# Attention block: the normalised output is stored one key step later, and one weight preparation step per quad is left out

## The chip, the cores and the metric

The kernel runs on one core of one Trainium2 chip. The metric is the device time of one execution in microseconds, the median over several runs. Lower is better. The names of the engines are those of the profile: PE (TensorE) does the matmuls, DVE, ACT and POOL are the vector, scalar and general engines, and SP issues every DMA of this program.

## What is computed

A transformer block with adaptive layer norm: multi-query attention (32 query heads of 18 columns, one key and one value head) and an MLP, over 2048 tokens of 576 features, in fp32.

```
mod = (silu(c) @ w_mod).reshape(c.shape[0], 6, 1, -1)
sa, ca, ga, sb, cb, gb = (mod[:, 0], mod[:, 1], ..., mod[:, 5])
h = layernorm(x) * (1 + ca) + sa
x = x + ga * A(h)      # q,k,v = h@wq, h@wk, h@wv; p = softmax(q k^T * 18**-0.5); (p v) @ wo
h = layernorm(x) * (1 + cb) + sb
x = x + gb * B(h)      # gelu(layernorm(h) @ w1 + b1) @ w2 + b2, with 4608 hidden features
```

## The kernel before

**Stages.** Stage 1 (up to about 134 us) projects q, k and v. Stage 2 (134 to 1422 us) is attention. Stage 3 (1422 us to the end) first adds the output projection of the last 512 tokens and then runs the MLP in 36 passes `v`.

**Quads and key steps.** Attention goes over 32 quads `n`: 4 blocks of 512 tokens times 8 groups `qd` of four heads. A quad has 16 key steps `kc` of 128 keys. For each key step PE makes the scores (L824), ACT takes their exponentials into a tile `P` (L826), and PE multiplies by the values (L813) into the PSUM tile `psC`. In between PE computes the plain scores of a later quad once more (L322, L834) so that DVE finds each query's maximum (L846, L844). Those maxima of quad n+1 are gathered at key steps 12 and 13 of quad n (`smax_fin1`, `smax_fin2`). `smax_fin2` writes them into a small tile `ms`, and four DMAs (L367) put `ms` as extra rows into the query tile `qst` of quad n+1. The first score matmul of quad n+1 reads `qst`. These four DMAs are called the ms DMAs below.

**What sets the order.** The order on each engine is the order in which the code calls it; nothing is reordered by a scheduler. `between(n, kc)` is called once after each key step, and draws one step of several Python generators, in this order: `smax_fin1` or `smax_fin2`, then the `post_quad` of the quad before (in the list `posts`), the load of a later quad's queries, on odd key steps a step of `fill` (output projection and second layer norm of finished token blocks), and last a step of `prep`.

**post_quad.** When quad n is done, its output goes from PSUM to a tile `O` (L619, ACT). In the key steps of quad n+1 the four softmax sums are fetched out of `O` by DMA (L637, tile `R`), inverted (L641), sent to DRAM (L643, `dsum`) and read back broadcast over the partitions (L647, tile `T`). At key step 8 POOL multiplies `O` by `T` (L651). At key step 9 POOL splits the product into two parts in the tile `os` (L661, L662). Some key steps later four DMAs store `os` into `ATT` (L668, `big<-os`), the left operand of the output projection (L597). Four heads of quad 30 lie in chunk k = 3 of `ATT` for the last token block. Quads 0 to 2 and 31 take another path, without these sums by DMA.

**prep.** From quad 3 on, `prep` draws one step of `weight_parts` per key step. It scales w2 (L728), makes sums of w1 and w2 blocks (L730, L754), and splits each into two parts in a tile `r2`, of which there are two buffers (L694 and L695, the function `two`). The DMA that stores a split (`store`, L699) is issued when the next step is drawn. The blocks of w2 are loaded by L705 (tiles `r4` and `w2b`), and those of w1 for four of the 18 groups by L739 and L741 (tiles `r1` and `r4`; `r1` shares its memory with `w2b`). At key step 8 of quad 31 a loop draws whatever is left of `prep`, and then the first MLP weights are loaded (`load_w1`, L683, eight DMAs into `w1a`).

**The end of attention.** After the last quad PE runs `wo_tile` for three token tiles with k = 0 to 3 (L597), and then the last chunk and the first MLP products (L1040).

Of the kernel before, what the change touches and what calls it, by code (L numbers as in the profile page):

```python
# [30 lines left out]
def block_kernel(ctx: ExitStack, tc, x, wqkv, wo, w1, b1, w2, b2, c, wmod, ident_in, out):  # L31
# [277 lines left out]
    def load_q(n):  # L309
        tb, qd = divmod(n, NQ)  # L310
        if n not in QST:
            new_q(n)
        q = QST[n]
        for g in range(2):
            for r in range(3):
                src = qscr[tb, r // 2, 4 * DH * qd:4 * DH * (qd + 1), :]
                src = src.rearrange("(p g d) t -> g d p t", p=2, g=2)[g]
                sy.dma_start(q[64 * g + DH * r:64 * g + DH * (r + 1)].bitcast(F32), src)
# [30 lines left out]
    def smax_fin1(n):  # L349
        m = MR[n] = pa.tile([128, 16], F32, name="mxf", bufs=2)  # L350
        mm = MX.pop(n)
        if n == 0:
            ve.tensor_reduce(m, mm, axis=AX.X, op=ALU.max)
        else:
            ve.tensor_reduce(m[:, :8], mm[:, :8, :], axis=AX.X, op=ALU.max)
            ve.tensor_reduce(m[:, 8:], mm[:, 8:, :3], axis=AX.X, op=ALU.max)

    def smax_fin2(n):
        p = psB()
        pe.transpose(p[:16, :128], MR.pop(n), ident)  # L360
        ms = pa.tile([16, 2, 128], F32R, name="ms")
        ac.activation(ms[:, 0], p[:16, :128], AF.Copy, scale=-1.0)
        ve.scalar_tensor_tensor(ms[:, 1], p[:16, :128], -1.0, ms[:, 0].bitcast(F32), op0=ALU.mult, op1=ALU.subtract)
        for g in range(2):
            for s in range(2):
                r = 64 * g + R3 + s
                sy.dma_start(QST[n][r:r + 1].rearrange("o p (t c) -> o (p t) c", c=128).bitcast(F32),  # L367
                             ms[8 * g:8 * (g + 1), s].bitcast(F32))
# [205 lines left out]
    def ln2_block(tb):  # L574
        if "b" not in B2:
            B2["b"] = b2_scaled(load_b2())
        if tb % 2 == 0:
            YR[tb // 2] = per.tile([128, 2 * KD, TB], F32, name="yr", tag="big", bufs=3)
        for t in range(NT):
            yield from ln2_tile(tb, t)  # L580
        if tb % 2:
            R = YR[tb // 2]
            po.tensor_tensor(R[:, 5:7], R[:, 7:9], R[:, 5:7], op=ALU.subtract)
            yield
            po.tensor_tensor(R[:, 5:7], R[:, 5:7], R[:, 0:2], op=ALU.add)
            yield
# [16 lines left out]
    def wo_block(tb):  # L603
        for t in range(NT):
            for h2 in range(2):
                p = psB()
                wo_mm(tb, t, h2, p, 0, KD)
                wo_add(tb, t, h2, p)
                yield
# [3 lines left out]
    def post_quad(n, PV):  # L613

        tb, qd = divmod(n, NQ)
        last = n == NQT - 1 or n < 3
        e = ve if n == NQT - 1 else po
        O = px.tile([128, TB], F32, name="O")
        ac.activation(O, PV, AF.Copy)  # L619
        yield  # L620
        if last:
            yield
            T = px.tile([128, 16, 32], F32, name="T")
            ve.transpose(T.rearrange("p a b -> p (a b)"), O)
            yield
            R = px.tile([128, 16], F32, name="R", bufs=2)
            ve.reciprocal(R, T[:, :, DH])
            e.tensor_tensor(T, T, R[:, :, None].to_broadcast([128, 16, 32]), op=ALU.mult)
            yield
            if e is po:  # L630
                yield
            ve.transpose(O, T.rearrange("p a b -> p (a b)"))
            yield
        else:
            R = px.tile([128, 16], F32, name="R", bufs=2)
            for j in range(4):
                sy.dma_start(R[32 * j:32 * (j + 1)], O[32 * j + DH:32 * j + DH + 1].rearrange("o (c i) -> o c i", i=16))  # L637
            yield
            yield
            yield  # L640
            ve.reciprocal(R, R)  # L641
            yield
            sy.dma_start(dsum[n % 2].rearrange("j (c i) -> (j c) i", i=16), R)  # L643
            yield
            T = px.tile([128, TB], F32, name="T")
            for j in range(4):
                sy.dma_start(T[32 * j:32 * (j + 1)], dsum[n % 2, j:j + 1].to_broadcast([32, TB]))  # L647
            yield
            yield
            yield  # L650
            po.tensor_tensor(O, O, T, op=ALU.mult)  # L651
            yield
        A = ATT[tb].rearrange("p (s k) t -> p s k t", s=2)
        if qd == NQ - 1:
            os = A[:, :, KD - 1, :]
        else:
            os = px.tile([128, 2, TB], F32R, name="os")
        if last:
            ac.activation(os[:, 0], O, AF.Copy)
        else:  # L660
            po.tensor_copy(os[:, 0], O)  # L661
        e.tensor_tensor(os[:, 1], O, os[:, 0].bitcast(F32), op=ALU.subtract)  # L662
        if qd < NQ - 1:
            for _ in range(3):
                yield
            for j in range(4):
                k, r = divmod(4 * qd + j, HC)
                sy.dma_start(A[DH * r:DH * (r + 1), :, k, :].bitcast(F32), os[32 * j:32 * j + DH].bitcast(F32))  # L668
        yield
# [8 lines left out]
    def load_w1(i, what, save=False):  # L678
        for w in what.split():
            a = 4 * OPS.index(w) if w in OPS else 28  # L680
            b = min(a + 4, 31)
            ends = W1["r"][:, a:b].bitcast(F32), w1scr[i, :, a:b]
            sy.dma_start(*(ends[::-1] if save else ends))  # L683
# [108 lines left out]
    def step(q):  # L792
        if q:
            try:
                next(q[0])
            except StopIteration:
                q.popleft()
# [8 lines left out]
    def pv_mm(n, kc, h0, h1):  # L806

        if kc == 0 and h0 == 0:
            PVt[n] = psC()
        t = P.pop((n, kc)) if h1 == 4 else P[n, kc]  # L810
        cs = slice(128 * h0, 128 * h1)
        for j in range(4):
            pe.matmul(PVt[n][32 * j:32 * (j + 1), cs], V[:, kc, :], t[:, j, cs],  # L813
                      start=(kc == 0 and h0 == 0), stop=(kc == 15), skip_group_check=True)
        if kc == 15 and h1 == 4:
            gen = post_quad(n, PVt.pop(n))
            next(gen)
            posts.append(gen)
# [29 lines left out]
    def between(n, kc):  # L848

        if kc == 12 and n + 1 < NQT:  # L850
            smax_fin1(n + 1)
        if kc == 13 and n + 1 < NQT:
            smax_fin2(n + 1)
        for gen in list(posts):
            if next(gen, 0) == 0:
                posts.remove(gen)
        if kc == 1 and n >= 1 and n + 2 < NQT:
            load_q(n + 2)
        if kc == 12 and n % NQ == 0 and n:
            fill.append(wo_block(n // NQ - 1))  # L860
            if n // NQ - 1 < 2:
                fill.append(ln2_block(n // NQ - 1))
        if kc % 2:
            step(fill)
        if n > 2 and kc not in (11, 12):
            step(prep)
        if kc == 8 and n == NQT - 1:
            while prep:
                step(prep)
            W1["r"] = per.tile([128, 40, 128], F32R, name="w1a", tag="big", bufs=3)  # L870
            load_w1(0, " ".join(OPS) + " tails")

    for d in range(8 * NQT):
        n, kd = divmod(d, 8)
        if kd == 0 and n % NQ == 0:
            ATT[n // NQ] = big()
        un = units.get(d)
        ns, nm, np_ = [0, 0], [0, 0], 0
        for tok in MIX if un else PLAIN:
            if tok in "PH":  # L880
                s, h0 = 2 * d + np_ // 4, np_ % 4
                np_ += 4 if tok == "P" else 2
                if s:
                    pv_mm(*divmod(s - 1, 16), h0, (np_ - 1) % 4 + 1)
                if np_ % 4 == 0:
                    between(n, s % 16)
                continue
            g = int(tok[1])
            if tok[0] == "s":
                st_mm(n, 2 * kd + ns[g] // 2, g, ns[g] % 2)  # L890
                ns[g] += 1
            else:
                mx_mm(*un, tok[0], g, nm[g])
                nm[g] += tok[0] == "m"
# [469 lines left out]
```

## Time and profile before

| | |
|---|---|
| median of 3 runs | 2301.75 us (2300.64 to 2305.29) |
| the profiled execution | 2300.77 us, span 2299.0 us |
| PE busy | 2261.0 us, 98% of the span |
| DVE, ACT, POOL busy | 1685.6, 1486.5, 1351.4 us |
| mean granted clock of PE | 0.998 |

Times in the profile are microseconds from the start of the span. In a row of the timeline stand the start, the duration, the engine (SPq is SP issuing a DMA), the line of the code, the operation, the tile written and the tiles read, and in brackets how long the engine had been idle and what ended that. In a row of waits stand the total, the number of times and the longest. In a row of windows stand the length, the busy time of an engine with its number of instructions in brackets, the granted clock as a share of the full one, and the DMA engines' share.

### The profile page before, as it was taken

Reading aid. Unit: us, or ns where it says so; the run is one execution under the profiler, and the core shown is the slowest. Engines: PE = TensorE matmul, PEld = TensorE weight load, DVE = VectorE, ACT = ScalarE, POOL = GpSimd, SP = SyncE. Lnnn points to the kernel's source line nnn. Section 1 sums busy time; section 2 is a strip of 40 time slices with the busy share of each in tenths; the row PEclk is TensorE's granted clock in tenths of the full one; section 3 lists DMA queues with packets and bytes.
Section 4 is the critical chain, followed back from the end, with each engine's and each line's share of the span. In section 5 each row is a group of like instructions: output and inputs, shape, how many; then the busy total and the mean of one; then the engine's idle time right before and its main releaser. Section 6 shows DMA issues by size and latency. Waiting matters only on the chain.

```text
span 2299.0 us, 44576 instructions
## 1 busy us (share of the span) xinstructions
PE 2261.0 (98%) x16310; PEld 1414.3 (62%) x16310; DVE 1685.6 (73%) x3004; ACT 1486.5 (65%) x2851; POOL 1351.4 (59%) x1554
## 2 busy tenths in 40 slices
PE   8999999999999999999999999999999999999999
PEld 5644434454344454344454344899999999989898
DVE  6589999979899979999879992444444456666665
ACT  5569999979999969999979998322222232222221
POOL 6534556345566425657324332588888767777776
PEclk9999999999999999999999999999999999999999
DMA  6221223222222212223123232444444456666663
GB/s 221 87 99 48 76 88 108 89 81 66 75 79 83 92 55 84 83 69 104 60 64 98 73 97 83 162 153 172 149 153 172 147 165 194 181 177 184 178 183 124
DMA packets 160411, 267.73 MB, mean 116 GB/s; under 512 B 26955, under 2 KB 67787, under 8 KB 160193
## 3 DMA queue, kind: packets, MB, share of 16 engines
q1 hardware_dynamic: 160193, 264.89, 36.7%
q8 instruction: 129, 2.11, 0.4%
q14 instruction: 89, 0.73, 0.1%
HBM read 163.45 MB, written 92.24 MB: 111 GB/s over the span
## 4 chain that ended last, share of the span: by engine, by line
PE 92%; ACT 2%; issue 0%; DVE 0%; DMA 0%; SPq 0%; POOL 0%; ACTq 0%
PE psC L813 24%; PE psB L1040 18%; PE psB L824 12%; PE psA L1151 10%; PE psM L322 10%; PE psA L1120 8%; PE psB L834 4%; PE psB L597 2%; ACT P L826 1%; ACT O L619 1%; PE psA L597 1%; PE psB L152 0%; PE psB L251 0%; PE psB L360 0%; DMA qst<-ms 0%
## 5 line engine op out<-in xcount | busy, mean ns | idle before, releaser
L826 ACT ACTIVATE P<-psB 128x512 f32<-128x512 f32 x2048 | 1048.8, 617 | 7.7 <-PE psB L824 6.4
L846 DVE TENSOR_REDUCE mx<-psM 128x1 f32<-128x512 f32 x1476 | 945.6, 683 | 72.1 <-PE psB L824 28.2
L813 PE MATMUL psC<-P,V 128*32 128x256 f32 (+1 forms) x6056 | 599.4, 467 | 13.2 <-ACT O L619 13.2
L824 PE MATMUL psB<-qst,KS 64*128 64x512 f32 x2048 | 598.6, 435 | 5.1 <-DMA qst<-ms 4.7
L322 PE MATMUL psM<-KS,qst 64*128 64x512 f32 x1722 | 592.2, 432 | 0.0
L824 PEld LDWEIGHTS psB<-qst,KS 64*128 64x128 f32 x2048 | 301.3, 185 | 174.4 <-issue 77.6
L1040 PE MATMUL psB<-ops,w1a 128*128 128x512 f32 x1512 | 390.6, 396 | 0.0
L322 PEld LDWEIGHTS psM<-KS,qst 64*128 64x128 f32 x1722 | 283.9, 185 | 115.2 <-DVE mx L844 92.6
L1040 PEld LDWEIGHTS psB<-ops,w1a 128*128 128x128 f32 x1512 | 271.6, 188 | 47.7
L813 PEld LDWEIGHTS psC<-P,V 128*32 128x32 f32 x6056 | 119.7, 108 | 236.9 <-issue 212.1
L1151 PE MATMUL psA<-w2s,big 128*128 128x288 f32 x1488 | 255.4, 295 | 0.0
L1055 ACT ACTIVATE yr<-psB,b1t 128x512 f32<-128x512 f32 x72 | 49.6, 689 | 287.2 <-PE psB L1040 147.1
L1151 PEld LDWEIGHTS psA<-w2s,big 128*128 128x128 f32 x1488 | 221.3, 188 | 6.7
L837 ACT ACTIVATE xc<-psB 128x512 f32<-128x512 f32 x246 | 147.5, 600 | 90.8 <-PE psM L322 61.6
L1155 DVE TENSOR_TENSOR XT<-psA,XT 128x576 f32<-128x576 f32 x152 | 114.2, 752 | 121.5 <-PE psA L1151 121.4
L1055 ACT ACTIVATE gx<-psB,b1t 128x512 f32<-128x512 f32 x72 | 49.6, 689 | 225.8 <-PE psB L1040 76.5
L844 DVE CUSTOM_DVE_ANT_0 xc<-psM,xc 128x512 f32<-128x512 f32 x246 | 167.0, 679 | 4.1 <-PE psM L322 3.4
L1126 DVE TENSOR_TENSOR XT<-psA,XT 128x576 f32<-128x576 f32 x170 | 128.7, 757 | 32.8 <-PE psA L1120 23.5
L834 PEld LDWEIGHTS psB<-KD,qst 64*128 64x128 f32 x246 | 45.1, 183 | 159.2 <-ACT P L826 109.8
L132 POOL MEMSET qst<- 32x1024 f32 x62 | 58.6, 946 | 137.2 <-PE psB L824 91.8
L1059 POOL TENSOR_TENSOR big<-gx,big 128x512 fp32r<-128x512 f32 x72 | 94.8, 1316 | 63.4 <-ACT big L1058 49.6
L834 PE MATMUL psB<-KD,qst 64*128 64x512 f32 x246 | 122.4, 498 | 0.0
(197 smaller groups left out, 2978.1 us busy)
## 6 DMA issues: line engine op xcount, KB each, us to landing
w1a<-w1scr SPq DMA_DIRECT2D x154, 256.0 KB
w1scr<-w1a SPq DMA_DIRECT2D x98, 256.0 KB
w2scr<-r SPq DMA_DIRECT2D x72, 288.0 KB
w2sum<-r SPq DMA_DIRECT2D x68, 288.0 KB
w2s<-w2sum SPq DMA_DIRECT2D x68, 288.0 KB
w2s<-w2scr SPq DMA_DIRECT2D x29, 576.0 KB
qst<-qscr SPq DMA_DIRECT2D x192, 72.0 KB
w2s<-w2scr SPq DMA_DIRECT2D x34, 288.0 KB
```

The costliest lines, as they stand in the source:

```text
L322: pe.matmul(o, QST[n][64 * g:64 * g + 64, p, 128 * qt:128 * (qt + 1)], KS[64 * g:64 * g + 64, 512 * kb:512 * (kb + 1)], start=True, stop=True)
L813: pe.matmul(PVt[n][32 * j:32 * (j + 1), cs], V[:, kc, :], t[:, j, cs], start=(kc == 0 and h0 == 0), stop=(kc == 15), skip_group_check=True)
L824: pe.matmul(t, KS[64 * g:64 * g + 64, 128 * kc:128 * (kc + 1)], QST[n][64 * g:64 * g + 64, i, :], start=True, stop=True)
L826: ac.activation(P[n, kc][:, 2 * i + g, :], t, AF.Exp, scale=SCALE)
L834: pe.matmul(t, QST[n][64 * g:64 * g + 64, p, 128 * qt:128 * (qt + 1)], KD1[64 * g:64 * g + 64, :], start=True, stop=True)
L837: ac.activation(XC[-1], t, AF.Relu)
L844: ve.tensor_tensor_reduce(c, t, c, 1.0, -3.0e38, ALU.add, ALU.max, o)
L846: ve.tensor_reduce(o, t, axis=AX.X, op=ALU.max)
L1040: pe.matmul(o, x, y, start=(first and i == 0), stop=(i == len(terms) - 1), skip_group_check=True)
L1120: pe.matmul(p[:, i, :288], x[:, ts_], W2S[k][:, y], start=(bool(first) and q == 0), stop=(q == 2), skip_group_check=True)
L1126: ve.tensor_tensor(o, p[:, :, :288], o, op=ALU.add)
L1151: pe.matmul(p[:, nn, :288], x, y, start=(q == 0), stop=(q == len(terms) - 1))
```

## The change

The generator `post_quad` yields four times instead of three between the split and the store for n > 2, so the four `big<-os` DMAs are issued at key step 13 instead of 12. Since `smax_fin2` runs ahead of `posts` at key step 13, its ms DMAs now stand ahead of them on SP. And `prep` is no longer drawn at key step 10, as it was not at 11 and 12 before.

```diff
@@ post_quad
         if qd < NQ - 1:
-            for _ in range(3):
+            for _ in range(4 if n > 2 else 3):
                 yield
             for j in range(4):
...
@@ between
-        if n > 2 and kc not in (11, 12):
+        if n > 2 and kc not in (10, 11, 12):
             step(prep)
         if kc == 8 and n == NQT - 1:
             while prep:
                 step(prep)
```

In the rows of the order below an engine's instructions stand as they are queued: line, operation, output<-inputs, shape, and xN for several in a row. A number after `r_` is a buffer's number and means nothing else.

SP, ahead of quad 12 (key steps 8 to 15 of quad 11), before:

```order
L647 DMA T<-dsum 32x512 x4
L699 DMA w2scr<-r_8013 256x1x288
L699 DMA w2sum<-r_8085 128x576
L699 DMA w2scr<-r_8161 256x1x288
L668 DMA big<-os 18x2x512 x4
L367 DMA qst<-ms 1x8x128 x4
L699 DMA w2sum<-r_8308 128x576
L637 DMA R<-O 32x1x16 x4
```

And now:

```order
L647 DMA T<-dsum 32x512 x4
L699 DMA w2scr<-r_8066 256x1x288
L367 DMA qst<-ms 1x8x128 x4
L668 DMA big<-os 18x2x512 x4
L699 DMA w2scr<-r_8142 256x1x288
L699 DMA w2sum<-r_8331 128x576
L637 DMA R<-O 32x1x16 x4
```

The ms DMAs have moved ahead of the four stores of `os` and of the prep store that was drawn at key step 10. It is the same ahead of quads 5 to 31, ahead of quad 20 with the same rows, save where the last head group of a token block (`qd` = 7) has nothing to store.

POOL, in quad 31, from the multiplication of quad 30 (key step 8) to its split (key step 9), before:

```order
L651 TENSOR_TENSOR O<-O,T 128x512
L773 TENSOR_TENSOR r_19579<-r_19577 128x128
L775 CAST r_19995<-r_19577 128x256
L776 TENSOR_TENSOR r_19995<-r_19577,r_19995 64x256
L775 CAST r_19995<-r_19579 128x128
L776 TENSOR_TENSOR r_19995<-r_19579,r_19995 64x128
L661 CAST os<-O 128x512
L662 TENSOR_TENSOR os<-O,os 128x512
```

And now, the first twelve rows from the same multiplication on:

```order
L651 TENSOR_TENSOR O<-O,T 128x512
L694 CAST r_19932<-w2b 128x288
L695 TENSOR_TENSOR r_19932<-w2b,r_19932 128x288
L728 TENSOR_TENSOR w2b<-w2b,BC 128x576
L694 CAST r_19941<-w2b 128x288
L695 TENSOR_TENSOR r_19941<-w2b,r_19941 128x288
L728 TENSOR_TENSOR r_19936<-r_19936,BC 128x576
L694 CAST r_19946<-w2b 128x288
L695 TENSOR_TENSOR r_19946<-w2b,r_19946 128x288
L694 CAST r_19950<-r_19936 128x288
L695 TENSOR_TENSOR r_19950<-r_19936,r_19950 128x288
L694 CAST r_19954<-r_19936 128x288
```

After these come the L695 of the last split, seven splits of 256 columns with four L754 between them, and the five rows L773 to L776 of before, and only then L661 and L662. Between L651 and L661 stood 5 instructions, and now stand 35.

SP, at the same place, before (from the sums of quad 30 to the stores of its `os`):

```order
L643 DMA dsum<-R 128x16
L699 DMA w1scr<-r_19889 128x512
L647 DMA T<-dsum 32x512 x4
L699 DMA w1scr<-r_19934 128x512
L699 DMA w1scr<-r_19973 128x512
L699 DMA w1scr<-r_19995 128x384
L683 DMA w1a<-w1scr 128x512 x7
L683 DMA w1a<-w1scr 128x384
L668 DMA big<-os 18x2x512 x4
```

And now:

```order
L699 DMA w2sum<-r_19932 128x576
L705 DMA r_19936<-in_w 128x576
L705 DMA w2b<-in_w 128x576
L699 DMA w2scr<-r_19941 256x1x288
L699 DMA w2scr<-r_19946 256x1x288
L699 DMA w2scr<-r_19950 256x1x288
L699 DMA w2scr<-r_19954 256x1x288
L739 DMA r_19958<-in_w 128x1024
L741 DMA r_19960<-in_w 128x256
L699 DMA w1scr<-r_19963 128x512
```

Behind these ten rows stand the other seven w1scr stores, and then, as before, the eight L683 loads and the four stores of `os`. The loads of the last group's w2 and w1 (L705, L739, L741), which were issued in quads 29 and 30, now stand here.

## The prediction

> **What bounds the kernel now.** I read the page first, then the waits of PE, then windows around each wait, then the timeline of SP and POOL at two places. PE carries the span:
>
> ```profile
> span 2299.0 us, 44576 instructions
> PE 2261.0 (98%) x16310; PEld 1414.3 (62%) x16310; DVE 1685.6 (73%) x3004; ACT 1486.5 (65%) x2851; POOL 1351.4 (59%) x1554
> PE 92%; ACT 2%; issue 0%; DVE 0%; DMA 0%; SPq 0%; POOL 0%; ACTq 0%
> ```
>
> PE idles 2299.0 - 2261.0 = 38.0 us in all. Whatever the change does to POOL and SP counts only where PE comes to wait, or no longer waits. Of PE's waits one group ends with the landing of the ms DMAs, and windows show two of its three and what the clock did:
>
> ```profile
> PE psB L824 <- DMA qst<-ms: 4.7, 3, 2.3
> ...
> 617.00:619.27 2.27, 0.00 (x1) 1.00 0.16 56
> 620.70:624.20 3.50, 3.50 (x22) 0.51 0.00 0
> 132.70:139.50 6.80, 6.41 (x26) 0.50 0.51 147
> 945.00:949.60 4.60, 2.58 (x21) 1.00 0.17 37
> ```
>
> In the first window PE stands still for 2.27 us (ahead of quad 12). In the last it is busy 2.58 of 4.60 us, so it stands still 2.02 us (ahead of quad 20). The third is the rest, 4.7 - 2.27 - 2.02 = 0.4 us, small beside them. The second window shows PE at half clock for 3.5 us soon after the first wait, and the third shows 6.8 us at half clock at the start of attention. Nothing like it follows the 2.02 us wait.
>
> After attention nothing gives time back: PE is busy 839.79 of 840 us there.
>
> ```profile
> 1450.00:2290.00 840.00, 839.79 (x5007) 759.00 (x5006) 456.52 (x648) 213.60 (x346) 634.19 (x693) 1.00 0.53 166
> ```
>
> **Part 1: ms DMAs ahead of the stores, no prep store ahead of them from key step 10.** SP and POOL ahead of quad 12:
>
> ```profile
> 600.62 0.34 SPq L699 DMA_DIRECT2D w2sum<-r  x1
> 611.07 0.52 SPq L699 DMA_DIRECT2D w2scr<-r  x1
> 611.65 3.44 SPq L668 DMA_DIRECT2D big<-os  x4
> 615.19 2.80 SPq L367 DMA_DIRECT2D qst<-ms  x4
> ...
> 604.49 2.30 POOL L538 TENSOR_SCALAR Z<-XT,mv,rs 128x576 f32<-128x576 f32 x1
> 608.37 1.42 POOL L540 TENSOR_TENSOR Z<-Z,BC 128x576 f32<-128x576 f32 x1
> 610.24 0.81 POOL L695 TENSOR_TENSOR r<-r,r 128x288 fp32r<-128x288 f32 x1
> ```
>
> A layer norm step (L538 to L540) holds POOL from 604.49 to 609.79. The prep split behind it ends at 611.05, and only then can SP issue its store at 611.07. Four stores of `os` follow for 3.44 us, and the ms DMAs start at 615.19. With the change the last thing ahead of the ms DMAs is the store of the split that POOL made ahead of the layer norm; its like was issued at 600.62 here. So 0.52 + 3.44 us of SP and the wait for POOL leave the path. That is more than the 2.27 us that PE waits, and I take both waits as gone: 2.27 + 2.02 = 4.29 us. The half clock after the longer one goes with it: 3.5 us at half speed cost 3.5 x 0.49 = 1.7 us. Together -6.0 us. The ends are 0, if `ms` itself is as late, and -6.0, since no other wait of PE has to do with these queues.
>
> What comes late instead are the stores of `os`. Behind them on SP is the prep store and the fetch of the next sums (L637), which must wait for the next `O` anyway. `ATT` is read quads later, so they cost nothing, except at the end of attention, which is part 2.
>
> The Trainium skill ("TensorE: Matmul & The Clock Gate", "The HAM clock gate") says that the clock falls to half after an idle window of about 3.4 us. Here a wait of 2.27 us was followed by half clock, so the trace shows less than that to be enough. If the rule were strict, the fall would not be due to the wait, and the gain would be 4.3 us; that is a rival below.
>
> **Part 2: one step of prep less per quad.** Quads 3 to 30 each draw 13 steps instead of 14. That leaves 28 steps more to the loop at key step 8 of quad 31. The order shows it: between L651 and L661 of quad 30's output stand 35 POOL instructions instead of 5. The two splits of `os`, the w1 loads and the four stores of `os` are queued behind all of that, on POOL and on SP. PE reads these stores with the tenth matmul after attention (three each for k = 0 to 2, then k = 3). This end looked so before:
>
> ```profile
> 1401.00 1.28 POOL L651 TENSOR_TENSOR O<-O,T 128x512 f32<-128x512 f32 x1
> 1402.24 0.46 POOL L773 TENSOR_TENSOR r<-r 128x128 f32<-128x128 f32 x1
> 1404.82 0.61 POOL L661 CAST os<-O 128x512 fp32r<-128x512 f32 x1
> ...
> 1405.15 3.77 SPq L683 DMA_DIRECT2D w1a<-w1scr  x8
> 1409.02 3.43 SPq L668 DMA_DIRECT2D big<-os  x4
> ...
> 1422.14 6.64 PE L597 MATMUL psA<-wos,big 126*128 126x288 f32 x48
> ...
> DMA  0000983999989999998997655410000000000000
> ```
>
> The last row is the DMA engines' busy share from 1404 to 1420 us in 40 slices of 0.4 us. It falls to zero after slice 27, so everything has landed at 1404 + 27 x 0.4 = 1414.8. PE needs it at 1422.14 + 9 x 6.64/48 = 1423.4. The slack was 8.6 us. A delay D of this group makes PE wait D - 8.6 us.
>
> What the added instructions take comes from these rows:
>
> ```profile
> 1338.63 1.41 POOL L728 TENSOR_TENSOR r<-r,BC 128x576 f32<-128x576 f32 x1
> 1359.97 0.42 POOL L694 CAST r<-r 128x288 fp32r<-128x288 f32 x1 [18.68 <-DMA w2scr<-r]
> 1361.22 0.42 POOL L694 CAST r<-r 128x288 fp32r<-128x288 f32 x1
> 1370.36 0.40 POOL L694 CAST r<-r 128x256 fp32r<-128x256 f32 x1
> 1371.51 0.40 POOL L694 CAST r<-r 128x256 fp32r<-128x256 f32 x1
> 1396.85 0.74 POOL L754 TENSOR_TENSOR r<-r,r 128x256 f32<-128x256 f32 x1
> 1397.65 0.40 POOL L694 CAST r<-r 128x256 fp32r<-128x256 f32 x1
> ```
>
> A split of 288 columns takes 1361.22 - 1359.97 = 1.25 us, one of 256 columns 1.15, an L754 0.80, an L728 1.41. Added are 5 x 1.25 + 2 x 1.41 + 7 x 1.15 + 4 x 0.80 = 6.3 + 2.8 + 8.1 + 3.2 = 20.3 us of POOL alone (the five rows L773 to L776 were there before). No step can hide in another, as it is one engine's queue.
>
> To that come waits that this burst can't avoid. The w2 blocks of the last group are loaded inside it, and then those of w1, which go where w2 was:
>
> ```profile
> 1332.57 0.44 SPq L705 DMA_DIRECT2D w2b<-in_w  x1
> 1335.88 1.41 POOL L728 TENSOR_TENSOR w2b<-w2b,BC 128x576 f32<-128x576 f32 x1 [2.29 <-DMA w2b<-in_w]
> ...
> 1243.52 0.42 SPq L705 DMA_DIRECT2D w2b<-in_w  x1
> 1248.46 1.42 POOL L728 TENSOR_TENSOR w2b<-w2b,BC 128x576 f32<-128x576 f32 x1 [11.16 <-DMA w2b<-in_w]
> ...
> 306.88 0.42 SPq L739 DMA_DIRECT2D r<-in_w  x1
> 307.35 0.43 SPq L741 DMA_DIRECT2D r<-in_w  x1
> 311.09 0.40 POOL L694 CAST r<-r 128x256 fp32r<-128x256 f32 x1 [5.48 <-DMA r<-in_w]
> ```
>
> A w2 load takes 3.3 to 4.9 us from its issue until POOL goes on, and SP issues a store and the other load ahead of it for 0.8 us: 4.1 to 5.7 us, I take 4.8. A w1 load takes 311.09 - 306.88 = 4.2 us, and 0.4 us for the last store ahead: 4.6; up to 1 us more under load, I take 4.9. And each split needs one of two buffers, which is free once the store of the split before last has landed:
>
> ```profile
> 1371.59 0.33 SPq L699 DMA_DIRECT2D w1scr<-r  x1
> ...
> 1373.64 0.40 POOL L694 CAST r<-r 128x256 fp32r<-128x256 f32 x1 [0.92 <-DMA w1scr<-r]
> ```
>
> That is 2.05 us. Where two splits follow each other without other work, POOL waits 2.05 - 1.15 = 0.9 us at the second; this happens twice (the fourth split of w2, the third of w1), so 1.8 us, and 3.5 if a store takes 0.6 us more and four places wait. The sums of quad 30 come later by up to 1 us, because SP now issues stores of `os` ahead of the fetch (0.5 taken). D = 20.3 + 4.8 + 4.9 + 1.8 + 0.5 = 32.3 us, between 20.3 + 4.1 + 4.6 + 1.8 = 30.8 and 20.3 + 5.7 + 5.6 + 3.5 + 1 = 36.1. PE waits 32.3 - 8.6 = 23.7 us (22.2 to 27.5). Then the clock: two stretches of half clock are shown, 3.5 and 6.8 us, which cost 1.7 and 3.4 us. A wait ten times as long as the one at 617 may well cost the longer one; I take the middle, 2.6 us.
>
> **Sum.** -6.0 + 23.7 + 2.6 = +20.3 us. The profiled execution took 2300.77 us, so 2321.1; it lies 1.0 us below the median of 2301.75, so the median becomes about 2322. A difference of 0.2% is 4.6 us here, about what a measurement of this kernel can tell from no change.
>
> **The rivals.**
> - *The burst is covered.* If PE did not need the stores until the burst is over, only the gain would remain: 2301.75 - 6.0 = 2295.8. For that D must be below 8.6 us, and below 14.6 us to break even. The 20.3 us of POOL work alone are more, so this needs an error in the dependency: that the matmul with k = 3 does not wait for quad 30's heads. Chance 0.04; between the two, within 0.2%, 0.02.
> - *The gain of part 1 doesn't come.* The ms DMAs would wait for something else, most likely a late load or store of prep whose phase has shifted against the quads. For it: PE reaches the next quad soon after these DMAs everywhere. Against it: fewer items stand ahead of them. The time is 2301.75 + 23.7 + 2.6 = 2328. Chance 0.13.
> - *The half clock at 620 us has another cause* and stays: 2322 + 1.7 = 2323.7. The Trainium skill's rule on the clock, cited above, leads to this time. The 2.27 us wait just ahead of it speaks against this. Chance 0.06.
> - *The burst is slower than its parts*, because each store, load and split is chained through two buffers and SP: D about 40 us, PE waits 31 us, 2329. The low shares of the DMA engines at that place speak against it. Chance 0.07.
> - My forecast, 2322: 0.68. Its own range is 2319.7 (22.2 + 1.7 - 6.0 = +17.9) to 2326.7 (27.5 + 3.4 - 6.0 = +24.9).
>
> Faster by over 0.2%: 0.04. Within: 0.02. Slower: 0.94. The range of 2313 to 2330 leaves out the first rival and the far ends. It goes below 2319.7 because the waits that I added up for loads and buffers (4.8 + 4.9 + 1.8 = 11.5 us) could partly overlap; were half of it hidden, it would be 2316.
>
> **What the profile after would show.** The waits of PE: no L824 behind `qst<-ms` over 0.5 us, and a new one, L597 behind a DMA `big<-os`, once, about 24 us. POOL: 35 instructions between L651 and L661 of quad 30, L661 about 32 us later against the last quad's matmuls. SP: L683 and the last L668 as much later. PEclk: half for a few microseconds after that wait, and full at 620 us. I am wrong if PE goes from L813 to L597 without a stop, if waits for `qst` turn up in other quads, or if the MLP after 1450 us takes another time than before.

## The result and the profile after

The changed kernel takes 2322.76 us (median of 6 runs) against 2301.56 us before (6 runs): ratio 1.0092, 95% interval 1.0078 to 1.0105. It is slower by 21 us. One of its six runs took 4129.36 us, with nothing on record to explain it; the ratio leaves it out, and the median of the other five is 2322.02 us. The profiled execution took 2326.19 us, with a span of 2324.4 us, so its own difference to the profiled execution of before is 25.4 us.

The waits of PE, in total, number of times and longest:

```profile
PE psA L597 <- DMA big<-os: 27.5, 1, 27.5
PE psC L813 <- ACT O L619: 13.4, 30, 0.5
...
PE psB L824 <- DMA qst<-ms: 0.7, 1, 0.7
```

The waits for the ms DMAs fell from 4.7 to 0.7 us, and one new wait of 27.5 us stands at the output projection. The timeline of PE, then of POOL, then of SP at that place:

```profile
1417.31 1.46 PE L597 MATMUL psA<-wos,big 126*128 126x288 f32 x9
1446.30 7.74 PE L597 MATMUL psA<-wos,big 126*128 126x288 f32 x39 [27.52 <-DMA big<-os]
...
1398.52 1.28 POOL L651 TENSOR_TENSOR O<-O,T 128x512 f32<-128x512 f32 x1 [2.76 <-DMA T<-dsum]
...
1405.25 1.42 POOL L728 TENSOR_TENSOR w2b<-w2b,BC 128x576 f32<-128x576 f32 x1 [4.20 <-DMA w2b<-in_w]
...
1413.24 0.42 POOL L694 CAST r<-r 128x288 fp32r<-128x288 f32 x1 [1.30 <-DMA w2scr<-r]
...
1419.40 0.40 POOL L694 CAST r<-r 128x256 fp32r<-128x256 f32 x1 [4.87 <-DMA r<-in_w]
...
1422.69 0.40 POOL L694 CAST r<-r 128x256 fp32r<-128x256 f32 x1 [0.94 <-DMA w1scr<-r]
...
1434.64 0.61 POOL L661 CAST os<-O 128x512 fp32r<-128x512 f32 x1
...
1434.97 3.77 SPq L683 DMA_DIRECT2D w1a<-w1scr  x8
1438.84 3.47 SPq L668 DMA_DIRECT2D big<-os  x4
```

PE does nine matmuls, stops, and goes on when the stores of quad 30 have landed. From L651 to L661 POOL now needs 36.1 us; before it was 3.8.

The windows show where the clock was (length, busy time of PE with its instructions, granted clock, share of the DMA engines, GB/s). First three windows of after:

```profile
617.00:640.00 23.00, 22.61 (x199) 1.00 0.38 122
1446.30:1451.50 5.20, 5.20 (x22) 0.50 0.15 34
1451.50:1456.00 4.50, 4.50 (x36) 1.00 0.00 0
```

Then the stretch from the output projection to the end, in the windows of before:

```profile
1422.10:2299.00 876.90, 872.63 (x5213) 1.00 0.53 164
```

And in those of after:

```profile
1417.30:2324.40 907.10, 875.15 (x5213) 0.98 0.51 164
```

The half clock near 620 us is gone, and a new one of 5.2 us follows the long wait. From the output projection to the end it takes 907.1 - 876.9 = 30.2 us more. The matmuls of attention run from 135.2 us (the first L824 below) to 1417.3:

```profile
L824 PE MATMUL psB<-qst,KS x2048: 382/394/792, 135.2 to 1414.2; 64*128 64x512 f32 x187
```

Before it was 134.4 to 1422.1. So attention shrank from 1287.7 to 1282.1 us. In sum -5.6 + 30.2 = +24.6 us, and 0.8 us is a later start of attention, in a stage that the change doesn't touch (over the profiles of all the kernels shown here this start lies between 132.5 and 135.8 us): 25.4 us, all of the profiled difference.

### The profile page after: what moved, and what is told of

The parts are those of the page before. It is cut to its first block, busy times and chain, and to the rows that moved or that the text cites. A ratio compares the mean times of both kernels' runs of the same rounds, so it can differ in the third digit from the quotient of the medians.

```text
span 2324.4 us, 44596 instructions
## 1 busy us (share of the span) xinstructions
PE 2262.6 (97%) x16310; PEld 1419.1 (61%) x16310; DVE 1685.9 (73%) x3004; ACT 1486.0 (64%) x2851; POOL 1351.2 (58%) x1554
## 4 chain that ended last, share of the span: by engine, by line
PE 85%; POOL 3%; ACT 2%; DMA 2%; issue 1%; SPq 1%; DVE 0%; ACTq 0%; POOLq 0%
PE psC L813 20%; PE psB L1040 18%; PE psA L1151 10%; PE psB L824 10%; PE psM L322 10%; PE psA L1120 8%; PE psB L834 4%; PE psB L597 2%; ACT P L826 1%; DMA w1scr<-r 1%; POOL r L695 1%; ACT O L619 1%; PE psA L597 1%; SPq L668 1%; DMA big<-os 1%
## 5 line engine op out<-in xcount | busy, mean ns | idle before, releaser
L824 PE MATMUL psB<-qst,KS 64*128 64x512 f32 x2048 | 597.3, 435 | 1.1 <-DMA qst<-ms 0.7
L824 PEld LDWEIGHTS psB<-qst,KS 64*128 64x128 f32 x2048 | 301.2, 185 | 169.1 <-issue 72.4
```

The source lines that it names most:

```text
L824: pe.matmul(t, KS[64 * g:64 * g + 64, 128 * kc:128 * (kc + 1)], QST[n][64 * g:64 * g + 64, i, :], start=True, stop=True)
```

## The experiments

My theory: the gain is the ms DMAs that no longer stand behind stores, and the loss is the burst of left-over preparation steps in quad 31. Rival A: PE waits at the end because the stores of quad 30 are issued one key step later. Rival B: the gain comes from there being fewer preparation steps per quad.

**Only the later store.**

```diff
-            for _ in range(3):
+            for _ in range(4 if n > 2 else 3):
```

> Only the later store; key step 10 draws its preparation step as before, so 3 steps are left for quad 31. Theory (the gain is the ms DMAs that no longer stand behind the stores, the loss is the burst of left-over preparation steps): both waits of PE for qst and the half clock near 620 us are gone, no wait at L597, 2301.6 - 6 = about 2296. Rival A (PE waits at the end because the stores of quad 30 are issued one key step later): L597 waits as in the changed kernel and the time is 2320 or more. Rival B (the gain comes from fewer preparation steps per quad): the two waits for qst stay, about 2301.

Measured: 2294.82 us against 2301.25, ratio 0.997 (0.9958 to 0.9981). No wait at L597:

```profile
1416.52 6.64 PE L597 MATMUL psA<-wos,big 126*128 126x288 f32 x48
```

All 48 matmuls run in one piece. Rival A falls, since the later store alone costs nothing there, and rival B falls as the only cause, since the whole gain is there with the old number of steps.

**Only the step at key step 10 left out.**

```diff
-        if n > 2 and kc not in (11, 12):
+        if n > 2 and kc not in (10, 11, 12):
```

> Only the step at key step 10 left out; the stores stay at key step 12, ahead of the ms DMAs. Theory: the burst is there, L597 waits 25 to 28 us, then some 5 us at half clock, and since the late preparation store no longer holds the stores of os, the waits for qst are gone as well: about 2322, as the changed kernel. Rival A: no wait at L597, about 2301 or less. Rival B: the same time as the theory, so this run does not tell it apart.

Measured: 2320.13 us, ratio 1.008 (1.0067 to 1.0094).

```profile
PE psA L597 <- DMA big<-os: 24.6, 1, 24.6
PE psC L813 <- ACT O L619: 13.5, 30, 0.5
PE psB L824 <- DMA qst<-ms: 1.3, 2, 1.1
```

The loss comes with this part alone. The waits for `qst` are nearly gone here as well, so either part would have done for the gain. SP's rows ahead of quad 12 show how. With the later store alone the ms DMAs come right behind the preparation store that waited for POOL:

```profile
610.47 0.52 SPq L699 DMA_DIRECT2D w2scr<-r  x1
611.48 2.88 SPq L367 DMA_DIRECT2D qst<-ms  x4
```

With the preparation part alone they still stand behind the four stores of `os`, but these are issued 7 us earlier, as no late preparation store holds them:

```profile
603.62 3.42 SPq L668 DMA_DIRECT2D big<-os  x4
610.54 2.79 SPq L367 DMA_DIRECT2D qst<-ms  x4
```

Before, both stood in the way, one behind the other, and the ms DMAs were issued at 615.19. Neither alone makes PE wait there. So my theory as worded above, which names only the stores of `os`, has one half of it; the expectation for this run had the other. The wait of 24.6 us is just short of the 25 to 28 expected.

**The lost step drawn elsewhere.**

```diff
         if n > 2 and kc not in (10, 11, 12):
             step(prep)
+        if n > 2 and kc == 14:
+            step(prep)
```

> The changed kernel, with the step that key step 10 lost drawn at key step 14 (two steps there), so that 3 steps are left for quad 31 as before. Theory: the waits for qst are gone and so is the burst: 2296, faster than both kernels. Rival A: L597 still waits, 2320 or more. Rival B: the number of steps per quad is that of before, so waits for qst come back, 2301.

Measured: 2294.21 us, ratio 0.9968 (0.9957 to 0.998). With the later store and the same number of steps as before there is a gain and no loss. This and the first run are faster than both kernels, and don't differ from each other beyond the spread of their runs.

**Fewer steps left over.**

```diff
-        if n > 2 and kc not in (10, 11, 12):
+        if n > 2 and kc not in ((10, 11, 12) if n > 16 else (11, 12)):
             step(prep)
```

> The changed kernel, with key step 10 left out only from quad 17 on, so that 17 steps instead of 31 are left for quad 31 (23 POOL instructions between L651 and L661 instead of 35, and the loads of w2 outside the burst). Theory by the sum: 7 splits of 1.15 and 4 subtractions of 0.80 us added, about 1 us of waiting for the load of w1 and 0.9 for a buffer, L651 up to 2.4 us later: a delay of 13 to 16 us, less 7.8 us of slack: L597 waits 5 to 8 us, then half clock worth up to 2.6 us; with the gain of 6 us the time is 2301 to 2306. Rival A: L597 waits as long as in the changed kernel, 2322.

Measured: 2304.62 us, ratio 1.0013 (1.0004 to 1.0022).

```profile
PE psA L597 <- DMA big<-os: 7.7, 1, 7.7
```

That is its row of PE's waits, and these are two of POOL's timeline, the first and the last of the burst's stretch:

```profile
1399.06 0.40 POOL L694 CAST r<-r 128x256 fp32r<-128x256 f32 x1 [2.31 <-DMA r<-in_w]
1414.42 0.61 POOL L661 CAST os<-O 128x512 fp32r<-128x512 f32 x1
```

The wait follows the length of the burst, as the sum has it (5 to 8 us expected). The w1 load is waited for 2.3 us instead of 1.

**The changed kernel again**, beside the next two.

> The changed kernel once more, beside the next two. Theory: L597 waits 25 to 28 us in this profile too and PE then has half clock for 3.5 to 6.8 us; 2322 to 2323. No theory expects another time.

Measured: 2323.63 us, ratio 1.009 (1.0073 to 1.0107). L597 waits 27.1 us in this profile.

**The clock after the wait.** Three kernels queue matmuls of the identity on PE, whose result nobody reads, ahead of the output projection, so that PE works while it would wait:

```diff
+    busy(208)
     for t in range(3):
         wo_tile(t, 0, KD - 1)
```

> The changed kernel with 208 matmuls of the identity by itself, whose result nobody uses, queued on PE ahead of the output projection; at 0.126 us each (2.27 us for 18 in the profile of before) they fill 26.2 us of the wait of 27.5. Theory (the half clock after the wait costs 2.6 us of its own): the clock stays full there, L597 still waits some 1 to 2 us, and the time is 2.6 us shorter than that of the changed kernel, about 2320. Rival (the half clock costs nothing, since the wait for the stores is all): the same time within 0.5 us.

Measured: 2340.83 us, ratio 1.017 (1.0154 to 1.0185). The filler was mis-sized:

```profile
1417.96 46.72 PE L406 MATMUL psB<-ident 128*128 128x128 f32 x416
```

One such matmul is two entries of 0.112 us each, and my 0.126 us was for one entry. So PE worked 46.7 us and never waited. That is still of use: the clock stayed full, and from the output projection to the end it took as long as before the change:

```profile
1464.40:2341.40 877.00, 872.60 (x5215) 1.00 0.51 164
```

With 114 instead:

> The run before with 114 matmuls of the identity instead of 208. The first try filled 46.7 us instead of 26.2, because each such matmul is two entries of the profile, of 0.112 us: 114 of them fill 25.6 us, less than the wait of 27.5. Theory (the half clock after the wait costs 2.6 us of its own): the clock stays full, L597 waits some 0.5 to 2 us, and from the end of the last quad to the end of the program it takes 907.0 - 2.6 = 904.4 us; the time is about 2320.5. Rival (the half clock costs nothing): 907.0 us there, 2323.

Measured: 2324.84 us, ratio 1.0096 (1.0079 to 1.0112). The stores came later in this profile, so 3.47 us of waiting remained, and the clock fell for that too:

```profile
1439.72 1.44 PE L597 MATMUL psA<-wos,big 126*128 126x288 f32 x9
1444.63 7.89 PE L597 MATMUL psA<-wos,big 126*128 126x288 f32 x39 [3.47 <-DMA big<-os]
```

And in the window behind it:

```profile
1444.60:1450.10 5.50, 5.47 (x23) 0.50 0.11 35
```

It didn't tell the two apart. With 126:

> The same with 126 matmuls of the identity (28.3 us at 0.2246 each). With 114 PE still waited 3.5 us and the clock fell all the same, so that run did not separate the two. Now L597 should wait under 2 us. Theory (the half clock costs 2.6 us of its own): no half clock there; the filler and what follows it take 28.3 + 876.9 us plus that wait, 905 to 907, against 907 to 908.7 before, and the time is 1 to 3 us below that of the changed kernel. Rival (the half clock costs nothing): 907 to 909 again.

Measured: 2323.15 us, ratio 1.0091 (1.0077 to 1.0105).

```profile
1443.02 1.44 PE L597 MATMUL psA<-wos,big 126*128 126x288 f32 x9
1444.87 5.42 PE L597 MATMUL psA<-wos,big 126*128 126x288 f32 x39 [0.41 <-DMA big<-os]
```

The clock stays full, and the 39 matmuls after the wait take 5.42 us, against 7.74 in the changed kernel and 7.89 with 114. So the half clock has a price of its own: 2.3 us on these rows alone. From the start of the filler (1414.86) to the end of the span (2320.7) it takes 905.8 us, within the 905 to 907 that were expected and 1.3 us less than the 907.1 without a filler. But the medians of the whole don't show it: 2323.15 is no shorter than 2322.76 and 2323.63, and the ratios to the kernel before are 1.0091, 1.0092 and 1.0090. The filler itself takes all but about 1 us of what it saves, and that is less than these medians tell. The expected time was missed.

**The burst behind the stores.** The same 31 steps, drawn at key step 14 of quad 31, after the stores of quad 30 and the loads of the first MLP weights:

```diff
-        if kc == 8 and n == NQT - 1:
+        if kc == 14 and n == NQT - 1:
             while prep:
                 step(prep)
+        if kc == 8 and n == NQT - 1:
             W1["r"] = per.tile([128, 40, 128], F32R, name="w1a", tag="big", bufs=3)
```

> The changed kernel with the same 31 steps drawn at key step 14 of quad 31 instead of 8, so that POOL splits quad 30's output, and SP stores it and loads the first MLP weights, ahead of the burst. Theory (place in the queue, not the work, is what costs): no wait at L597 for big<-os; the burst ends some 15 us after the last quad, where the tiles of the MLP's first operands reuse its buffers, so PE waits up to 9 us at L597 or L1040 for those, with up to 2.6 us of half clock: 2295 to 2306. Rival (the burst costs the same wherever it stands in quad 31): 2320 or more.

Measured: 2320.73 us, ratio 1.0081 (1.0066 to 1.0096). Here my theory falls and the rival holds. PE's waits:

```profile
PE psA L597 <- ACT big L659: 25.6, 1, 25.6
```

ACT's timeline (line numbers above 870 are one more than in the other kernels):

```profile
1414.27 0.60 ACT L619 ACTIVATE O<-psC 128x512 f32<-128x512 f32 x1 [1.18 <-POOL r L694]
1441.52 2.95 ACT L926 ACTIVATE ops<-yr 128x1024 fp32r<-128x1024 f32 x3 [26.65 <-DMA w1scr<-r]
...
1448.91 0.63 ACT L659 ACTIVATE big<-O 128x512 fp32r<-128x512 f32 x1 [2.73 <-DVE O L632]
```

The stores of quad 30 no longer hold PE; it does all its k = 0 to 3. But ACT then writes `ops`, the first operands of the MLP, into memory in which the burst's splits lay, and waits 26.65 us for the last store of the burst to land. Behind that on ACT is L659, the last head group's output, which PE reads next. The burst holds up PE by a second way almost as long as by the first. It also ended later than I expected, 25 us after the last quad's matmuls (1439.35 against 1414.1) instead of 15: POOL waited 7.95 us for the load of w2 and 3.43 us for a buffer. What costs is that it ends late, not only which queue it stands in.

The changed kernel has that second way too. There the copy of quad 31's output (L619) waits for POOL's last read of the only buffer `O`. What follows it, and what PE reads of it with the last chunk (ACT and DVE, then PE):

```profile
1436.63 0.60 ACT L619 ACTIVATE O<-psC 128x512 f32<-128x512 f32 x1 [20.35 <-POOL os L662]
...
1444.56 0.63 ACT L659 ACTIVATE big<-O 128x512 fp32r<-128x512 f32 x1 [2.73 <-DVE O L632]
...
1445.55 0.68 DVE L662 TENSOR_TENSOR big<-O,big 128x512 fp32r<-128x512 f32 x1
...
1457.05 1.76 PE L597 MATMUL psA<-wos,big 128*128 128x288 f32 x12
```

The last head group's output is there at 1446.23, and PE comes to it at 1457.05, so here the second way had 10.8 us to spare. An estimate shows what it would cost if only the stores came in time. Before the change PE came to the last chunk 9.7 us after its first L597 (1431.80 - 1422.14). Here that would be 1427.0, and L659 ends at 1445.19: a wait of some 18 us in place of the 27.5.

## Why the prediction was right, step by step

**The gain (part 1), forecast -6.0, was -5.6 us in the profile, and -6.4 in the medians of the kernel with the later store alone.** Both waits of 2.27 and 2.02 us went, and the half clock near 620 us went with them. So that half clock belonged to the wait of 2.27 us, and the rival in which it stays is wrong. That -5.6 comes so close to -6.0 is in part luck: 0.9 of it lies in quad 0, where the half clock at the start of attention, which the change doesn't touch, ended at 137.4 us instead of 139.5. From the start of quad 1 to the end of attention (173.00 to 1422.14 before, 172.85 to 1417.31 after) it is -4.7 us, and -4.8 with the later store alone. The waits there (4.3 to 0.7 us) and the clock (1.7 us) add up to 5.3; where the other 0.6 us went stays open. The part that I put at nothing was not quite nothing: a new wait of 0.7 us, ahead of quad 6. There the four stores of `os` follow the ms DMAs at once:

```profile
364.39 2.83 SPq L367 DMA_DIRECT2D qst<-ms  x4
367.32 3.44 SPq L668 DMA_DIRECT2D big<-os  x4
```

PE waited until 370.04 for a landing; before, with the same ms DMAs at the same time and no stores behind, it did not. But the stores can't be the whole reason. With the later store alone they follow the ms DMAs there too (at 366.56), and PE doesn't wait; with the preparation part alone no store of `os` follows, and PE waits 1.1 us. What delays this landing stays open. I had named waits for `qst` in other quads, and such a wait of over 0.5 us, as signs of being wrong: here is one, small as it is.

**The delay D, forecast 32.3, was 34.65 us.** Against the first L597, L661 stood at 1404.82 - 1422.14 = -17.32 before and at 1434.64 - 1417.31 = +17.33 after. Its parts: from L651 to L661 it took 36.12 - 3.82 = 32.3 us more, where 31.8 was forecast. The load of w2 cost 4.20 us of waiting (4.8 forecast), that of w1 4.87 (4.9), the two buffers 1.30 + 0.94 = 2.24 (1.8). The rest was the 20.3 us of POOL's work plus small gaps. What was too small is the start: L651 came 2.35 us later against the matmuls, not 0.5. The fetch of the sums (L637) was 0.85 us later, within the 1 us that I had allowed; the rest came on the way through `dsum` and `T`, for whose landing POOL waited 2.76 us.

**The slack, forecast 8.6, was 34.65 - 27.52 = 7.1 us.** I read the landing off the DMA engines' busy share, which ended 5.8 us after the first of the four stores was issued. The 0 in that row is rounded (the same view still has 15 GB/s in that slice, of 0.4 us). In the profile after PE went on 1446.30 - 1438.84 = 7.46 us after it, and 6.5 to 7.4 us after it in the five other profiles in which PE waits for these stores. So the end of the busy share in one execution fell short of the moment at which PE goes on in another. What fills the time in between no run shows.

**The wait, forecast 23.7 (22.2 to 27.5), was 27.5 and 27.1 in two profiles of this kernel, and 24.6 with the preparation part alone.** The two terms above explain the difference of 3.8 us: D was 2.35 us longer (34.65 - 32.3) and the slack 1.5 us shorter.

**The half clock, forecast 2.6, was 907.1 - 876.9 - 27.5 = 2.7 us**, 5.2 us at half speed. The size came out, the reason did not: I took a longer wait to cost more. After PE went on, half clock lasted 5.2 us behind the wait of 27.5, but 5.5 behind 3.47 and 6.2 behind the 7.66 of the kernel with fewer steps left over. What sets it is in the last section.

**The sum** was +20.3 forecast, +25.4 between the two profiled executions, and +21.2 between the medians. The profiled execution is 3.4 us above the median of its kernel. The second profile of this kernel is 1.8 us shorter, and 1.6 us of that lie ahead of the output projection, 1.3 of them already at the start of attention; why, stays open. So the forecast of the median is closer than its terms deserve: the gain and the clock came out, the wait in the profile was 3.8 us longer.

**What the prediction didn't see** is the second way by which the burst holds up PE. It made no difference to the time here, as it had 10.8 us to spare. But the reason that I gave for break-even, that only the dependency at k = 3 stood between the burst and PE, was wrong, as the last experiment shows.

## What to carry to other kernels

When background work is drawn a step at a time and a loop empties the rest at the end, count the steps: leaving out one per round piles up all of them where nothing hides them any more. Here one step in each of 28 quads became 31 steps at once instead of 3, and cost 30 us against a gain of 6. When two small edits are made together, look for the one that already carries the gain: the later store alone gave 6.4 us and cost nothing.

## What the runs showed of the hardware that was not expected

- A wait of 2.27 us was followed by 3.4 us of half clock, one of 3.47 us by 5.5 us after PE went on, and one of 27.5 us by 5.2; a wait of 2.02 us and one of 0.41 us by none. The Trainium skill ("TensorE: Matmul & The Clock Gate", "The HAM clock gate") gives an idle window of about 3.4 us; the wait of 2.27 us is shorter than that, and the clock fell all the same.
- The clock changed only on a fixed grid of 3.413 us. In every profile here each stretch of half clock that the windows show, but for one that begins at the very end of the program, lasts a whole number of these intervals: 3.41 and 6.83 us before, 6.83 and 30.72 in the changed kernel, 10.24 with fewer steps left over, 27.31 with the burst behind the stores. Two stretches of one profile stand whole intervals apart too: in the changed kernel they end at 137.35 and 1451.48, which is 385 intervals. So how long the half clock lasts after PE goes on depends on where in an interval that is. In the changed kernel PE went on at 1446.30, inside the interval that ends at 1448.07, and full clock came at 1451.48, after the first interval that PE filled.
- It is the busy time in an interval that fits here, more than the length of the wait. These are the interval ahead of the half clock at 620.76, and the two around the wait of 2.02 us, counted on from there, all in the kernel before (length, busy time of PE with its matmuls, clock, DMA share, GB/s):

```profile
617.35:620.76 3.41, 1.49 (x13) 1.00 0.23 89
945.02:948.44 3.42, 2.55 (x17) 1.00 0.23 49
948.44:951.85 3.41, 2.26 (x23) 1.00 0.25 88
```

The clock fell after the first of them. The wait of 2.02 us lies across the boundary of the other two, and after neither did it fall. No run moves a wait against the grid to test this.

- A 128x128 fp32 matmul of the identity is two entries in the profile, 0.112 us each (46.72 us for 208 matmuls, 416 entries).
